# PSUM as one tile of eight banks and a new order of the same operations in a fused attention and MLP-mixer kernel

## The chip, the cores and the metric

One core of a Trainium2 chip runs the kernel. The metric is the device time of one execution in microseconds (us), the median over several runs. The engines are TensorE (PE, with its weight loads shown apart as PEld), VectorE (DVE), ScalarE (ACT), GpSimd (POOL) and SyncE (SP). Each works through its own list of instructions in order. DMA transfers are issued from POOL, SP and ACT.

## What is computed

Causal attention over blocks of 64 positions, then a mixer of tokens and channels, for 8 batches, 8 heads, 576 positions and 64 values per head (so a model width of 512):

```python
scores = scale * np.matmul(q, k.transpose(0, 1, 3, 2))     # block-causal mask: block_i >= block_j
attn = np.exp(scores - max); attn = attn / sum
x = np.matmul(attn, v)                                      # to (batch, 576, 512)
...
h = np.maximum(xt @ w_tok1, 0.0) @ w_tok2                   # over positions, 576 -> 256 -> 576
u = x + h.transpose(0, 2, 1)
h2 = np.maximum(u @ w_ch1, 0.0) @ w_ch2                     # over channels, 512 -> 1536 -> 512
return u + h2
```

Inputs and output are float32; the matmuls are in bfloat16.

## The kernel before

**The work.** For each batch the kernel makes `qT` and `kT` by 32x32 transposes on DVE, then for each half of the heads (`hg`, four heads) three score sets (`score_set`, L539, matmuls at L562), exponentials out of PSUM on ACT (L580 for two banks at once in the first batch, L736 and L777 for one bank), clears of masked parts (`clear`, L594, memset at L599) and a copy of the tail block (`tail`, L584), both on DVE or POOL. `head_out` (L605) multiplies by v for one head (L616) and divides on DVE (L636, L642); `ends_out` (L653) does the last 64 positions of two heads (L669, L691, L697). `token_up` (L805, L814 and L818) and `token_mix` (L888, L913 and L944), in the first batch `first_u` (L838), are the token mixer. The channel mixer's first product is plain for batch 0 (`channel_up`, L1041). For the other batches it saves one of eight block products (`channel_up_half` L1114, `channel_up_fast` L1238). There a first product goes to a bank, a copy on ACT or DVE (`seed`, through `cast` at L393 or L395) sets a second bank to the same values, and later products are added on in both. The second channel product is `first_down` (L1463) for batch 0 and `channel_down_fast` (L1372) for the rest; its results are added up by `fold` on DVE (L1396) and stored by SP or ACT (L1424 and L1438). The last 64 positions of all batches are gathered as one more batch, number 8, here called the mixed rows; its four stores are those of L1424.

**The order.** Nothing is scheduled at run time. `Plan.add` collects 1526 operations with their dependencies, and the table `ORDER` lists them as words: the operation's number, a letter for the engine (T, A, D, P, S), and, for a TensorE operation that opens banks, a letter for each place in PSUM. `Plan.placed` walks the table, and each operation issues its instructions on the engine named, so the table is the order on every engine. An operation that waits holds up all behind it on that engine.

**PSUM.** It has eight banks. Before, four are single tiles `mm` (letters a to d), and four are at first two pairs `sc` (s and t) that the first batch's score sets take whole. After the last exponential of the first batch the pairs are closed and reopened as four single tiles `late` (e to h). A bank's letter moves between named pools (`TURN`), which say whether the bank's last use wrote all of it (`covers`); a seeded bank that is not covered gets one more matmul (`cover`, L310).

**The start.** `raise_clock` (L358) runs 11 matmuls on zeros before anything has been loaded (L364), and then single filler matmuls, up to 37 of them, placed by the table where TensorE would wait (L372); 25 are in the table. POOL issues the loads of q, k and v of batch 0 (v in two halves, `load_v`, L456, one half for each four heads, in five pieces J of 128 positions, the last of 64), of batch 1's q and k (L417), of the token weights (`load_token_weights`, L477: `w1_sb` in two pieces, `w1o_sb`, `w2_sb`, issued at L480) and of the channel weights (L503, L512).

Of the kernel before, what the change touches and what calls it, by code (L numbers as in the profile page):

```python
# [9 lines left out]
FP32 = mybir.dt.float32  # L10
# [17 lines left out]
class Plan:  # L28


    TURN = {
        (pool, covers): to
        for pools in (("mm", "full"), ("late mm", "late"))
        for covers, to in zip((False, True), pools)
        for pool in pools
    }

    ENGINE = {"T": "PE", "A": "ACT", "D": "DVE", "P": "POOL", "S": "SP"}  # L40
    SLOTS = {
        **{letter: ("mm", n) for n, letter in enumerate("abcd")},
        **{letter: ("late", n) for n, letter in enumerate("efgh")},
        "s": ("sc01", 0), "t": ("sc23", 0),
    }

    def __init__(self):
        self.ops = []
        self.free = {}

    def pool(self, name, tiles):
        self.free[name] = list(range(len(tiles)))

    def add(
# [7 lines left out]
        o.emit, o.prio, o.take, o.give, o.xfer = emit, prio, take, give, xfer  # L62
# [6 lines left out]
    def bare(self, note):  # L69
        return note.get("seed", False) and note["pool"] in ("mm", "late mm")  # L70

    def placed(self):

        pool_of = {letter: pool for letter, (pool, _) in self.SLOTS.items()}
        held, done = set(), set()
        for word in ORDER.split():
            digits = word.rstrip("abcdefghstADPST")
# [4 lines left out]
            for letter, (pools, note) in zip(letters[1:], o.take):  # L82
                note["pool"], note["slot"], note["home"] = pool_of[letter], self.SLOTS[letter][1], letter
                assert letter not in held and note["pool"] in pools
                held.add(letter)
            yield o
            done.add(o.n)
            for note in o.give:
                if "home" not in note:
                    note["home"] = "efgh"[note["slot"]]  # L90
                else:
                    held.remove(note["home"])
                pool_of[note["home"]] = self.TURN.get((note["pool"], note.get("covers")), note["pool"])
# [4 lines left out]
    9D 8D 14S 7D 0A 15A 11S 41Ta 19P 69Tb 17P 1D 52Tb 21P 31P 25P 51Tb 65Tb 23P 29P 12A 27P 3D 2D 16D 20D 18D 22D  # L98
    13D 26D 24D 105Ts 106A 98Ttbc 61Td 57Td 49Td 99A 100D 30D 63Td 118A 122Ts 70Td 123A 78Td 62Td 54Td 102Tt 103A
# [79 lines left out]
def kernel(  # L179
# [82 lines left out]
    late = []  # L262

    P = Plan()
    SC = ("sc01", "sc23")
    for name in SC:
        P.pool(name, [0])
    P.pool("mm", mm)
# [1318 lines left out]
```

## Time and profile before

| | |
|---|---|
| timed runs | 283.83 us median of 3 (283.75 to 284.11) |
| span of the profiled execution, first to last instruction | 282.2 us |
| granted TensorE clock, mean | 1.000 |
| DVE idle | 282.2 - 238.8 = 43.4 us |
| DMA | 31.75 MB, mean 112 GB/s, of it 17.64 MB by POOL's queue |

The page gives the span of the profiled execution alone; its time with what lies around the span is not listed, and the timed runs are other executions. Matmul rows on the page overlap, because a matmul is pipelined and its end is modelled: a row of 0.38 us stands for a matmul that holds TensorE for less. In the chain of waits a row such as "53.72 0.97 PE mm L913 x4" gives the start, the time until the next piece, the engine, the tile, the line and the number of instructions. In the timeline a bracket gives the idle time ahead and what ended it.

### The profile page before, as it was taken

What the parts mean: (1) busy time and instruction counts of PE and PEld (TensorE: products, weight loads), DVE (VectorE), ACT (ScalarE), POOL (GpSimd) and SP (SyncE); (2) the same over time, 40 slices, a digit from 0 to 9 for tenths busy, and PEclk for the clock granted to TensorE, in tenths of its full rate; (3) what the DMA queues carried; (4) which work ended last, traced back from release to release, by engine and by line L of the source; (5) the groups of instructions that cost most, each with busy time, mean ns of one, the idle gap of its engine ahead of it and who ended that gap; (6) DMA issues with size and microseconds to landing.
All of it is one profiled execution on the core that took longest, in us unless ns stands there. A gap on an engine that the chain in (4) does not pass through costs nothing.

```text
span 282.2 us, 8544 instructions
## 1 busy us (share of the span) xinstructions
PE 275.3 (98%) x3580; PEld 193.2 (68%) x3580; DVE 238.8 (85%) x523; ACT 177.8 (63%) x326; POOL 78.8 (28%) x131
## 2 busy tenths in 40 slices
PE   7899999999999999999999999999999999999994
PEld 2457665475768877888776658744589664788884
DVE  4589598889889989999988879887797898898974
ACT  4788888775899774899997990326840858530000
POOL 8876726371613422092257210000000000000000
PEclk9999999999999999999999999999999999999999
DMA  8999999959958947699399465150127200020555
GB/s 160 167 153 194 191 200 203 162 63 170 95 88 229 150 67 56 151 104 127 46 118 161 31 141 120 42 114 19 37 49 210 80 0 0 3 75 14 212 126 174
DMA packets 64918, 31.75 MB, mean 112 GB/s; under 512 B 53104, under 2 KB 56176, under 8 KB 64880
## 3 DMA queue, kind: packets, MB, share of 16 engines
q0 software_dynamic: 45040, 17.64, 54.0%
q1 hardware_dynamic: 19408, 12.91, 16.7%
q10 hardware_dynamic: 432, 0.66, 0.7%
q8 instruction: 28, 0.46, 0.7%
q14 instruction: 10, 0.08, 0.1%
HBM read 35.85 MB, written 9.44 MB: 160 GB/s over the span
## 4 chain that ended last, share of the span: by engine, by line
PE 82%; DMA 10%; DVE 3%; ACT 2%; POOL 1%; issue 1%; DVEq 0%; POOLq 0%
PE mm L1372 13%; PE late L1372 11%; DMA qk_sb<-in_q_dram 7%; PE late L1114 7%; PE late L1238 6%; PE mm L1114 6%; PE mm L1238 6%; PE mm L562 4%; PE late L616 3%; DMA wc_sb<-in_moe_w_ch_dram 3%; PE late L562 3%; PE late L913 3%; PE mm L814 2%; PE mm L616 2%; PE late L814 2%; PE mm L913 2%
## 5 line engine op out<-in xcount | busy, mean ns | idle before, releaser
L777 ACT ACTIVATE e_sb<-mm 128x512 bf16<-128x512 f32 x94 | 53.5, 612 | 9.8 <-PE mm L562 4.2
L777 ACT ACTIVATE e_sb<-late 128x512 bf16<-128x512 f32 x74 | 43.0, 613 | 5.6 <-PE late L562 2.7
L440 DVE STREAM_TRANSPOSE qk_sb<-qk_sb 128x288 int32<-128x288 int32 (+2 forms) x57 | 38.3, 695 | 6.0 <-ACT qk_sb L393 1.9
L469 POOL DMA_DIRECT2D vals<-in_v_dram x45 | 37.1, 833 | 8.5 <-PE late L616 7.5
L1372 PEld LDWEIGHTS <-sums 128*128 128x128 bf16 x288 | 27.8, 98 | 4.2 <-issue 0.4
L1372 PEld LDWEIGHTS <-gT 128*128 128x128 bf16 x288 | 27.9, 98 | 3.7
L562 PEld LDWEIGHTS <-qk_sb 32*64 32x64 bf16 (+1 forms) x1024 | 16.9, 99 | 16.5 <-issue 9.6
L562 PE MATMUL mm<-qk_sb 32*64 32x320 bf16 (+6 forms) x534 | 27.7, 273 | 0.0
L616 PEld LDWEIGHTS <-e_sb 128*128 128x128 bf16 x640 | 23.9, 97 | 5.4 <-issue 0.9
L393 ACT COPY late<-mm 128x512 f32<-128x512 f32 (+1 forms) x14 | 8.0, 571 | 27.6 <-DVE o_sb L1396 14.5
L562 PE MATMUL late<-qk_sb 32*64 32x320 bf16 (+6 forms) x382 | 25.0, 277 | 0.3 <-DVE x_sb L642 0.3
L1114 PEld LDWEIGHTS <-ws_sb 128*128 128x128 bf16 x192 | 17.9, 98 | 4.2 <-issue 0.9
L599 POOL MEMSET e_sb<- 64x512 bf16 (+1 forms) x23 | 11.4, 511 | 31.7 <-ACT e_sb L777 28.4
L800 ACT ACTIVATE gT<-late 128x512 bf16<-128x512 f32 x20 | 12.2, 611 | 7.4 <-PE late L1114 4.9
L1114 PEld LDWEIGHTS <-wc_sb 128*128 128x128 bf16 x144 | 15.5, 113 | 1.8
L1238 PEld LDWEIGHTS <-ws_sb 128*128 128x128 bf16 x96 | 9.4, 98 | 9.8
L616 PE MATMUL late<-vals,e_sb 128*128 128x65 bf16 x360 | 15.8, 193 | 0.0
L642 DVE TENSOR_TENSOR x_sb<-late,rinv 128x256 bf16<-128x256 f32 x36 | 14.8, 418 | 0.7
L580 ACT ACTIVATE e_sb<-sc 128x1024 bf16<-128x1024 f32 x11 | 10.8, 1026 | 4.5 <-PE sc L562 4.5
L1372 PE MATMUL mm<-wd_sb,sums 128*128 128x256 bf16 x108 | 13.1, 273 | 0.0
L616 PE MATMUL mm<-vals,e_sb 128*128 128x65 bf16 x280 | 12.4, 193 | 0.0
L417 POOL DMA_DIRECT2D qk_sb<-in_k_dram x12 | 6.6, 551 | 20.7 <-ACT e_sb L777 7.1
(203 smaller groups left out, 649.4 us busy)
## 6 DMA issues: line engine op xcount, KB each, us to landing
out_dram<-o_sb SPq DMA_DIRECT2D x14, 512.0 KB, 3.0
vals<-in_v_dram POOLq DMA_DIRECT2D x28, 128.0 KB, 5.9
qk_sb<-in_k_dram POOLq DMA_DIRECT2D x12, 288.0 KB, 5.6
qk_sb<-in_q_dram POOLq DMA_DIRECT2D x12, 288.0 KB, 6.1
wc_sb<-in_moe_w_ch_dram POOLq DMA_DIRECT2D x8, 192.0 KB, 7.8
wc_sb<-in_moe_w_ch_dram POOLq DMA_DIRECT2D x3, 512.0 KB, 8.0
out_dram<-o_sb SPq DMA_DIRECT2D x4, 256.0 KB, 3.2
vals<-in_v_dram POOLq DMA_DIRECT2D x15, 64.0 KB, 5.4
```

Of the source, the lines that this page charges most:

```text
L440: nc.vector.transpose(dst[:, 0:S, :] .rearrange("p s e -> p (s e)") .bitcast(I32) .rearrange("p (a k) -> p k a", k=NB)[:, k0:k1], raw2.bit ...
L469: nc.gpsimd.dma_start(out=t[128 - p : 128, J, hs, 0:64], in_=src)
L562: nc.tensor.matmul(out=home(n)[rows, c : c + w], lhsT=kT[i][r, 64 * j : 64 * j + keys, par], rhs=qT[i][r, 64 * q : 64 * q + w, par], start ...
L599: (nc.vector if o.engine == "DVE" else nc.gpsimd).memset(late_keys, 0.0)
L616: nc.tensor.matmul(out=u[:, I, 0:65], lhsT=e[:, h, c : c + 128], rhs=vt[:, J, head, 0:65], start=(J == 0), stop=(J == I),)
L642: nc.vector.tensor_tensor(out=xt[:, 0:4, 64 * head : 64 * head + 64], in0=u[:, :, 0:64], in1=ri[:, 0:4].to_broadcast([128, 4, 64]), op=MULT,)
L777: nc.scalar.activation(dst, bank_of(x), EXP, scale=scale)
L800: nc.scalar.activation(dst, src, RELU)
L913: nc.tensor.matmul(out=bank_of(bank), lhsT=w2_sb[:, t, 128 * si : 128 * si + 128], rhs=at[:, t, :], start=(t == 0), stop=(t == NDT - 1),)
L1114: nc.tensor.matmul(out=bank_of(bank)[:, 256 * o_ : 256 * o_ + 256], lhsT=x(o_, m), rhs=y[:, :, m, :], start=opens, stop=m == 1, skip_group ...
L1238: nc.tensor.matmul(out=bank_of(bank), lhsT=x(m), rhs=y[:, :, m, :], start=first and m == 0, stop=m == 1, skip_group_check=not first,)
L1372: nc.tensor.matmul(out=bank_of(bank)[:, 256 * i : 256 * i + 256], lhsT=x[:, kk, 128 * i : 128 * i + 128], rhs=y[:, kk], start=first and i ...
```

## The change

The eight banks become one tile, `banks_sb`, 128 x 8 x 512. A place in PSUM is now a first bank (letters a to h) and a size, 1 or 2, so that the first batch's pairs can lie on any two neighbouring banks and are given back one use at a time; the pools, the closing of the pairs and its dependency on the last exponentials go. Whether a bank is covered is kept in one set.

```diff
     def bare(self, note):
-        return note.get("seed", False) and note["pool"] in ("mm", "late mm")
+        return note.get("seed", False) and not note["whole"]
...
-            for letter, (pools, note) in zip(letters[1:], o.take):
-                note["pool"], note["slot"], note["home"] = pool_of[letter], self.SLOTS[letter][1], letter
-                assert letter not in held and note["pool"] in pools
-                held.add(letter)
+            for letter, (size, note) in zip(letters[1:], o.take):
+                note["slot"] = "abcdefgh".index(letter)
+                banks = range(note["slot"], note["slot"] + size)
+                assert banks.stop <= 8 and not held.intersection(banks)
+                note["whole"] = self.covered.issuperset(banks)
+                held.update(banks)
             yield o
             done.add(o.n)
-            for note in o.give:
...
+            for note, lo, hi in o.give:
+                banks = range(note["slot"] + lo, note["slot"] + hi)
+                held.difference_update(banks)
+                (self.covered.update if note["covers"] else self.covered.difference_update)(banks)
...
-    13D 26D 24D 105Ts 106A 98Ttbc 61Td 57Td 49Td 99A 100D 30D 63Td 118A 122Ts 70Td 123A 78Td 62Td 54Td 102Tt 103A
+    22D 13D 26D 24D 105Te 106A 98Tgbc 82P 30D 99A 102Td 34P 125Tf 118A 32P 119A 28D 158Ta 103A 122Tc 126A 104D
...
-    mm = ring(4, [128, 512], FP32, "mm", psum)
-    held_banks = [tc.tile_pool(name="pairs", bufs=1, space=bass.MemoryType.PSUM)]
-    sc = ring(2, [128, 2, 512], FP32, "sc", held_banks[0].__enter__())
-    late = []
+    banks_sb = psum.tile([128, 8, 512], FP32, name="banks")
...
-    def bank_of(note):
-        if note["pool"] in EARLY:
-            return mm[note["slot"]]
...
+    def bank_of(note, i=0):
+        return banks_sb[:, note["slot"] + i]
...
-            nc.scalar.activation(dst, sc[SC.index(note["pool"])][:, :, 0:n], EXP, scale=scale)
+            nc.scalar.activation(dst, banks_sb[:, note["slot"] : note["slot"] + 2, 0:n], EXP, scale=scale)
```

The operations and their dependencies are the same 1526, but for the dependency on the closing of the pairs. The table is another one throughout: 21 of the 25 filler matmuls are no longer in it, 37 evacuations go from ACT to DVE and 31 from DVE to ACT, and 13 copies and clears go from DVE to POOL and 11 from POOL to DVE. All else keeps its engine. The counts of matmuls are the same apart from the fillers. Three places, on engines that wait or are waited for, are shown.

POOL at the start, from the second piece of batch 0's loads on. `vals` is v (`4x64` are four heads, 64 rows the last piece), `gT` holds batch 1's raw q and k, `w_sb` and `w1o_sb` are token weights. Before:

```order
L469 DMA vals<-in_v_dram 64x4x64
L469 DMA vals<-in_v_dram 128x4x64 x3
L417 DMA gT<-in_q_dram 128x1152
L417 DMA gT<-in_k_dram 128x1152 x2
L469 DMA vals<-in_v_dram 64x4x64
L469 DMA vals<-in_v_dram 128x4x64 x4
L480 DMA w_sb<-in_moe_w_tok_dram 128x4x256
L480 DMA w_sb<-in_moe_w_tok_dram 64x256
L480 DMA w1o_sb<-in_moe_w_tok_dram 64x256
L599 MEMSET e_sb 64x2x2x64
```

and now:

```order
L450 DMA w_sb<-in_moe_w_tok_dram 128x4x256
L387 DMA gT<-in_q_dram 128x1152
L439 DMA vals<-in_v_dram 64x4x64
L439 DMA vals<-in_v_dram 128x4x64
L563 MEMSET e_sb 64x2x2x64
L450 DMA w_sb<-in_moe_w_tok_dram 64x256
L563 MEMSET e_sb 64x2x2x64
L439 DMA vals<-in_v_dram 128x4x64 x2
L552 COPY vals<-e_sb 128x128
L439 DMA vals<-in_v_dram 128x4x64
L450 DMA w_sb<-in_moe_w_tok_dram 128x1152
```

The five pieces of the second half of v stood together ahead of the token weights; now they stand behind the large piece of them, apart from each other, with two clears and a copy between that wait for exponentials. Ahead of what is shown, `w1o_sb` now stands before the first half's later pieces, and the identity matrix (masks.py) before `w_sb`.

SP at the end, its stores to the output. `64x2x512` are stores of the mixed rows (256 KB each), `128x512` and `128x256` are stores of batch 7 (256 and 128 KB). Before:

```order
L1438 DMA out_dram<-o_sb 128x2x512 x7
L1424 DMA out_dram<-o_sb 64x2x512 x3
L1438 DMA out_dram<-o_sb 128x256
L1438 DMA out_dram<-o_sb 128x512
L1438 DMA out_dram<-o_sb 128x256 x2
```

and now:

```order
L1399 DMA out_dram<-o_sb 128x2x512 x6
L1385 DMA out_dram<-o_sb 64x2x512 x2
L1399 DMA out_dram<-o_sb 128x256
L1385 DMA out_dram<-o_sb 64x2x512
L1399 DMA out_dram<-o_sb 128x256 x2
L1399 DMA out_dram<-o_sb 128x512
```

The third store of the mixed rows moves behind the first store of batch 7, and the store of 128x512 from third last to last place.

ACT at the end, its three stores. Before:

```order
L393 COPY mm<-mm 128x512
L393 COPY late<-mm 128x256
L1424 DMA out_dram<-o_sb 64x2x512
L1438 DMA out_dram<-o_sb 128x512
L1438 DMA out_dram<-o_sb 128x256
```

and now:

```order
L1245 ACTIVATE vals<-vals 128x2x512
L363 COPY banks<-banks 128x256
L1385 DMA out_dram<-o_sb 64x2x512
L1399 DMA out_dram<-o_sb 128x256
L1399 DMA out_dram<-o_sb 128x512
```

The 256 KB store of batch 7 and the 128 KB store have changed places. In the table the last five words on TensorE are 1521, 1500, 1511, 1517 and 1496, six matmuls each (L1372). The last fold of the mixed rows stands just ahead of them, the fold of 1517 frees ACT's last store, and that of 1496 SP's last store.

224 lines of the change are left out of this document (94 added, 130 removed).

## The prediction

> **What bounds the kernel now.** I read the page's shares first, then the windows by stage, the chain of waits, and the timeline of the first 24 and the last 10 us.
>
> ```profile
> PE 275.3 (98%) x3580; PEld 193.2 (68%) x3580; DVE 238.8 (85%) x523; ACT 177.8 (63%) x326; POOL 78.8 (28%) x131
> 8.50:22.00 13.50, 13.38 (x251) 7.51 (x253) 9.86 (x33) 11.53 (x13) 10.53 (x19) 1.00 1.41 164
> 22.00:60.00 38.00, 37.59 (x650) 23.76 (x647) 31.99 (x83) 32.08 (x63) 19.59 (x34) 1.00 1.26 173
> 60.00:110.00 50.00, 50.00 (x768) 36.57 (x761) 46.44 (x107) 37.52 (x72) 18.67 (x28) 1.00 1.01 129
> 110.00:165.00 55.00, 54.69 (x984) 40.63 (x982) 50.29 (x122) 48.23 (x94) 21.62 (x35) 1.00 0.79 100
> 210.00:260.00 50.00, 50.00 (x379) 37.68 (x377) 43.61 (x70) 23.23 (x41) 0.00 (x0) 1.00 0.19 56
> ```
>
> The columns are PE, weight loads, DVE, ACT, POOL, then the granted clock, the DMA share and GB/s. TensorE is busy in every stretch, at clock 1.00. So four things make the time: when the first useful matmul starts, how much matmul work there is, what PE loses between, and what follows the last matmul. A busy PE hides its waits, so the losses are read from the chain, where one operation stands many times:
>
> ```profile
> 53.72 0.97 PE mm L913 x4
> 205.45 0.86 PE mm L913 x4
> 92.77 0.56 PE late L1114 x4
> 94.64 0.44 PE late L1114 x4
> 277.96 0.69 PE mm L1372 x6
> 278.67 0.42 DVE o_sb L1396
> ```
>
> A group that had to wait costs about 0.11 us more than the same group unblocked. Adding up, over the PE rows of the timeline, each operation's start-to-start time less that of the faster quarter of its kind, I estimate some 5 us of such losses from 22 to 165 us and 0.3 us from 165 us to the last matmul, which ends at 278.65. From there to the end are 282.2 - 278.65 = 3.55 us. In the first 22 us ACT sets the pace:
>
> ```profile
> 5.95 1.03 PE L372 MATMUL mm<-wd_sb 128*128 128x512 bf16 x4
> 7.86 0.88 PE L562 MATMUL sc<-qk_sb 32*128 32x512 bf16 x6 [0.89 <-DVE qk_sb L440]
> 8.53 1.94 ACT L580 ACTIVATE e_sb<-sc 128x1024 bf16<-128x1024 f32 x2 [3.67 <-PE sc L562]
> 10.47 0.49 ACT e_sb L736
> 17.77 0.56 PE sc L562 x4
> 19.91 1.02 ACT L580 ACTIVATE e_sb<-sc 128x1024 bf16<-128x1024 f32 x1 [0.52 <-PE sc L562]
> 20.24 0.77 PE L616 MATMUL mm<-vals,e_sb 128*128 128x65 bf16 x20
> 20.85 0.49 PE L372 MATMUL mm<-wd_sb 128*128 128x256 bf16 x2
> 22.53 0.38 PE L814 MATMUL mm<-x_sb,w_sb 128*128 128x128 bf16 x4 [0.19 <-DVE x_sb L642]
> 23.09 0.39 PE L814 MATMUL late<-x_sb,w_sb 128*128 128x128 bf16 x4
> L372 PE MATMUL mm<-wd_sb 128*128 128x512 bf16 (+1 forms) x25 | 6.3, 344 | 0.0
> L580 ACT ACTIVATE e_sb<-sc 128x1024 bf16<-128x1024 f32 x11 | 10.8, 1026 | 4.5 <-PE sc L562 4.5
> ```
>
> **The change part by part.** *One PSUM tile.* It adds and removes no instruction, and each operation still reads and writes its own bank: 0. *21 warming matmuls fewer.* Four stay ahead of 7.86; the other 21 of the 25 stood where PE had nothing ready. What covers them is that wait itself, so 0; at most the pair at 20.85 held up the next score set, so a gain up to 0.4. *VectorE.* 37 evacuations move from ACT to VectorE and 31 back, 13 tail operations go to POOL and 11 come back: four more on VectorE, at 238.8/523 = 0.46 us each about 2 us. Its 282.2 - 238.8 = 43 us of idle time hide them: 0, and 2 us where that cover is gone.
>
> *The first batch.* The score sets now stand close together and take any two free banks, so ACT need not starve. From 8.53, eleven wide exponentials at 1.94/2 = 0.97 and two small ones at 0.49 end at 20.2, where before the last ended at 20.93. The next batch's two score sets wait for banks freed by the last two exponentials and end at about 20.8 (0.56 for a set, as at 17.77); two token-up groups follow (23.09 - 22.53 = 0.56 each), and head 4, which needs the second half of v, is due at 22.0. With v at hand PE would be about 1 us ahead there: before reaches the end of its second token-up group at 23.09 + 0.56 = 23.65, having done two heads (0.77) and two end groups more and one score set (0.56) less. But v is late:
>
> ```profile
> 8.81 0.55 POOL L417 DMA_DIRECT2D gT<-in_q_dram  x1
> 10.11 0.54 POOL L417 DMA_DIRECT2D gT<-in_k_dram  x1 [0.75 <-DMA qk_sb<-in_k_dram]
> 11.51 3.60 POOL L469 DMA_DIRECT2D vals<-in_v_dram  x5 [0.17 <-issue]
> 15.06 0.79 POOL L480 DMA_DIRECT2D w_sb<-in_moe_w_tok_dram  x1
> 18.82 0.31 POOL L599 MEMSET e_sb<- 64x256 bf16 x1
> vals<-in_v_dram POOLq DMA_DIRECT2D x15, 64.0 KB, 5.4
> qk_sb<-in_q_dram POOLq DMA_DIRECT2D x1, 64.0 KB, 4.2
> ```
>
> Before, the five loads are issued from 11.51 to 15.11; 5.4 us after the last issue, at 14.4, is 19.8, and head 4 starts at 20.24. In the new order one more load stands ahead of the two 288 KB loads (8.81 and 10.11 become about 10.1 and 10.8), and then POOL issues the identity (0.5), the weights (0.79) and another q load (0.56) before v's first two pieces (1.4). Two clears follow that wait for the fifth wide and the second small exponential (8.53 + 5 x 0.97 + 2 x 0.49 = 14.4), with the small weight load between them (0.31, 0.54, 0.31 and gaps): about 16.2. Two pieces of v, a copy, and the last piece follow, which is issued near 18.2. It lands at 22.4 with the 4.2 us of the quickest such load, at 23.6 with the median. The heads behind it on PE wait 0.4 to 1.6 us, and so do the multiplications on VectorE, the token-up groups and the first channel groups that they feed. Against the lead of 1 us that is -0.6 to +0.6 at the head; but the lead itself is given up at the same chain (last head, multiply, token-up, add, transpose), which before also set the pace up to 30 us. I take +0.6, bounds -1.0 (the lead is kept) to +2.0 (nothing of the wait is hidden and the loads are slower).
>
> *The middle.* The work is the same and everything is in another place, so before's rows give bounds only. The nearest are the 5 us of losses: a better order gains 3 of them, a worse one loses 2 more. What tips it is the seeded products (L1114, L1238). A first product is copied to a second bank, and only then do its followers go on.
>
> ```profile
> L393 ACT COPY late<-mm 128x512 f32<-128x512 f32 x13 | 7.6, 588 | 13.1 <-PE mm L1238 12.8
> L1238 PE MATMUL mm<-e_sb,ws_sb 128*128 128x512 bf16 x38 | 10.8, 379 | 0.0
> ```
>
> The copy takes 0.59 us, and the first product's result stands 0.379 - 0.216 = 0.16 after its slot: 0.75 before any queue. Before, nearly all followers come three products later (3 x 0.43 = 1.29); now some ten come two later (0.86), which leaves 0.1 us for an engine that is 63 or 85% busy. At 0 to 0.2 each I take +0.3 for the middle, bounds -3 to +2.
>
> *The tail.* The last PE work is the same six matmuls and one fold. What goes out after it differs:
>
> ```profile
> 278.00:280.00 2.00, 0.63 (x6) 0.32 (x4) 0.84 (x2) 0.00 (x0) 0.00 (x0) 1.00 0.75 263
> 268.21 4.53 SPq L1424 DMA_DIRECT2D out_dram<-o_sb  x3
> 279.13 0.34 ACTq L1438 DMA_DIRECT2D out_dram<-o_sb  x1
> out_dram<-o_sb ACTq DMA_DIRECT2D x2, 256.0 KB, 4.3
> out_dram<-o_sb ACTq DMA_DIRECT2D x1, 128.0 KB, 1.7
> out_dram<-o_sb SPq DMA_DIRECT2D x4, 256.0 KB, 3.2
> ```
>
> Before, the mixed rows' four stores (L1424) have been issued by 272.9 and the last is a 128 KB store at 279.13 that lands in 1.7 us. Now two of those 256 KB stores follow a fold only four short products (0.66 each) before the end, and the last two stores are of 256 KB, one per queue, issued at the last matmul's end and 0.5 us after it. In the last 2.5 us of matmuls and behind them 1408 KB go out, before 640 KB. At 263 GB/s the 768 KB more take 2.9 us, the upper bound; a 256 KB store that lands in 2 us instead of 1.7 gives +0.3. By the median of 3.2 against 1.7 it is +1.5, less a little overlap: I take +1.2.
>
> Sum: 0.6 + 0.3 + 1.2 = +2.1 on the span of 282.2, 284.3. The runs' median, 283.83, is 1.63 above that span; kept, the forecast is 285.9.
>
> **The rivals.** *Faster, a smoother middle:* ACT is nearly 2 us ahead after the first batch, and 3 of the 5 us from 22 to 165 go; with +0.2 from the start and +0.8 from the tail the span is 280.2, the time 281.8. For it: the losses come in quanta of 0.11 at hundreds of places. Against it: the followers that come closer. It decides if v's last piece lands before 22.4. *No change:* v is in time, the middle gains 1, the tail costs 1.2: about 284. *VectorE or the copies become the bound:* VectorE is 46.44 of 50 us busy from 60 to 110; if its 2 us more and the close followers show in full, the middle costs +2.3 instead of +0.3: 287.9. *The clock drops:* the 21 matmuls kept PE busy between 9 and 21 us.
>
> ```profile
> 1.66 4.45 PE L364 MATMUL mm<-wd_sb 128*128 128x512 bf16 x11 [1.66 <-DVE wd_sb L339]
> ```
>
> These eleven first matmuls took 4.45 us, 0.40 each against 0.86/4 = 0.216 later: a start at reduced rate costs 4.45 - 2.4 = 2.1 us. If the new gaps bring that back once, the time is 288.0. I see gaps of up to 1.8 us (score sets issued by 10.2, the next transposes done at 12.0), with work between them. The Trainium skill, page "TensorE: Matmul & The Clock Gate", section "Why this matters for your kernels", warns of PE gaps over some 3 us between bursts. By that rule gaps of this length keep the clock; no row of before shows a gap that long.
>
> **How the numbers follow.** A measurement of this kernel can tell 0.2%, 0.57 us, from no change. Forecast 0.48, with its own range 284.4 to 287.4; VectorE or the copies 0.14; the clock 0.06; no change 0.14; faster 0.18. Slower is 0.48 + 0.14 + 0.06 = 0.68. The faster case reaches below 282.6 and the two dear ones beyond 288.3 in about 1 in 10 each, so the range is 282.6 to 288.3.
>
> **What would show it.** Start: head 4's second half begins near 23.6 with PE idle ahead of it, and POOL issues the last piece of v near 18.2. Middle: the L913 and L1114 groups of 0.97 and 0.56 as often as before or more. Tail: the span ends about 4.7 us after the last matmul, and the last 256 KB store lands 3 us or more after its issue. Clock: any stretch after 8.5 below 1.00. The forecast is wrong if v's last piece has landed by 22.4, if the tail stays at 3.6 us, or if the losses from 22 to 165 fall below 3 us.

## The result and the profile after

The changed kernel takes 303.41 us (302.72 to 305.33, 4 runs) against 283.97 before (283.75 to 284.26, 4 runs): ratio 1.0694, 95% interval 1.0656 to 1.0733. It is 19.4 us slower. The forecast was 285.9 in a range of 282.6 to 288.3: right in sign, far off in size. One execution each of e2 (303.28 us) and e13 (309.35 us) ran more than 1.5% slower than the fastest of its kernel and is left out of the table below.

The page of the changed kernel: the span, the engines' busy time, PE's busy tenths and granted clock in 40 slices, the chain by engine.

```profile
span 300.8 us, 8507 instructions
PE 279.8 (93%) x3559; PEld 195.6 (65%) x3559; DVE 243.6 (81%) x527; ACT 175.6 (58%) x320; POOL 78.9 (26%) x133
PE   7899999999986499979999999999999999999991
PEclk9959999999999699999999999999999999999997
PE 78%; DVE 10%; DMA 6%; issue 2%; ACT 2%; DVEq 0%
```

Before, PE was 98% busy; now there is a hole in the 13th and 14th slice and a smaller one in the 18th, with a drop of the clock behind the first hole and another in the third slice. A transfer stands in the chain of waits with 6%. The windows around the holes (PE, weight loads, DVE, ACT, POOL, then clock, DMA share, GB/s), PE's waits (us in total, times, longest), and the pieces of the chain there:

```profile
80.00:90.00 10.00, 8.94 (x139) 6.37 (x137) 9.42 (x24) 8.30 (x18) 6.17 (x9) 1.00 0.65 79
90.00:100.00 10.00, 5.17 (x96) 4.03 (x94) 5.65 (x16) 5.63 (x11) 0.89 (x1) 0.98 2.16 120
100.00:110.00 10.00, 7.79 (x84) 5.62 (x85) 6.03 (x10) 3.94 (x8) 1.50 (x3) 0.68 0.97 41
130.00:140.00 10.00, 8.01 (x106) 6.86 (x104) 6.81 (x19) 7.24 (x15) 4.01 (x7) 1.00 1.27 135
```

```profile
PE banks L1075 <- DMA uT<-u_sb: 8.8, 2, 7.0
```

```profile
89.95 12.21 DMA uT<-u_sb
102.21 1.04 PE banks L1075 x4
...
128.01 6.64 DMA uT<-u_sb
```

From 96 us on all engines are idle together until 102 us, waiting for one transfer. It is a transpose through DMA. `token_mix` leaves u, the result of the token mixer, in `u_sb`; two transposing DMAs on SP's queue (L980 before, L941 now), one for each half, turn it into `uT`, the operand of the channel products (L1114 before, L1075 now). The first of batch 2 was issued at 85.42 and took 9.1 us; the second was issued at 89.95 and was 12.2 us on its way; that of batch 3 took 6.6. The landing times of all the transposes, before and then after:

```profile
DMA to landing us min/median/max: 3.0/3.2/4.6
```

```profile
DMA to landing us min/median/max: 3.2/5.6/12.2
```

What went on meanwhile is in the timeline of SP and of POOL, first after:

```profile
85.42 6.81 SPq L941 DMA_TRANSPOSE uT<-u_sb  x2
```

```profile
84.02 1.10 POOL L387 DMA_DIRECT2D qk_sb<-in_q_dram  x2 [0.83 <-DVE rinv L600]
85.10 0.55 POOL L563 MEMSET e_sb<- 64x512 bf16 x1
85.57 3.54 POOL L439 DMA_DIRECT2D vals<-in_v_dram  x4
89.06 0.61 POOL L387 DMA_DIRECT2D qk_sb<-in_k_dram  x1
94.70 0.89 POOL L439 DMA_DIRECT2D vals<-in_v_dram  x1 [5.03 <-PE banks L580]
```

and the same places before:

```profile
84.19 3.00 SPq L980 DMA_TRANSPOSE uT<-u_sb  x2
```

```profile
79.83 0.52 POOL L599 MEMSET e_sb<- 64x512 bf16 x1 [1.53 <-DVE vals L588]
89.33 0.52 POOL L599 MEMSET e_sb<- 64x512 bf16 x1 [8.97 <-ACT e_sb L777]
89.84 0.53 POOL L417 DMA_DIRECT2D qk_sb<-in_k_dram  x1
```

Before, POOL sat 9 us in front of a clear that waited for ACT, and the queue behind it was still; in that quiet the two transposes went through in 3.2 us. Now POOL issues four 128 KB pieces of v and a 288 KB piece of k from 85.6 to 89.7, and the second transpose comes right behind them. What the DMA engines moved from 93 to 95 us, packets and MB by queue (q0 is POOL's, q1 SP's), and what SP's queue moved from 84 to 103 us:

```profile
DMA packets 2342, 0.29 MB, mean 147 GB/s; under 512 B 2342, under 2 KB 2342, under 8 KB 2342
q0 software_dynamic: 2336, 0.29, 298.6%
q1 hardware_dynamic: 6, 0.00, 1.1%
```

```profile
q1 hardware_dynamic: 2112, 0.52, 36.4%
```

From 93 to 95 us the pieces of v move, in packets that are all under 512 B, and six packets of SP's queue. The 2112 packets are those of the two transposes, 1056 each. Of them 1056 moved before 95 us and 1056 after, so the six are the end of the first transpose (landed at 94.5), and the second, issued five us earlier, had not moved a packet by 95.

**The end** is longer too. The chain's last piece shows the last matmul at 267.09 + 27.52 = 294.6, so 6.2 us to the end of the span, against 3.55 before:

```profile
267.09 27.52 PE banks L1333 x252
```

**Two numbers for each run.** The time from the program's start to the first channel product of batch 0 (below: start) varies between executions of one and the same kernel, so the runs are compared by what lies behind it as well (below: rest, span less start). The start is read from the line of the tile `uT`, here for two executions of the changed kernel, 29.8 and 31.3 us:

```profile
L1002 PE MATMUL banks<-uT,wc_sb x48: 376/379/407, 29.8 to 46.3; 128*128 128x512 bf16 x48
```

```profile
L1002 PE MATMUL banks<-uT,wc_sb x48: 376/379/407, 31.3 to 47.8; 128*128 128x512 bf16 x48
```

| kernel | median us (lowest to highest, runs) | start | rest |
|---|---|---|---|
| before | 283.97 (283.75 to 284.26, 4) | 29.9 | 252.3 |
| changed | 303.41 (302.72 to 305.33, 4) | 29.8 | 271.0 |
| changed, again (e17) | 303.90 (302.95 to 305.95, 4) | 31.3 | 271.5 |
| e1 one tile, old order | 285.09 (284.13 to 285.84, 10) | 30.1 | 253.3 |
| e2 five loads behind | 299.05 (296.79 to 300.72, 3) | 30.1 | 267.1 |
| e4 before, loads early | 285.02 (1) | 29.9 | 253.3 |
| e5 u early | 298.33 (1) | 31.3 | 265.1 |
| e6 four pieces of v behind | 295.65 (294.47 to 296.25, 4) | 31.8 | 260.9 |
| e7 fillers back | 302.91 (301.37 to 304.50, 4) | 32.0 | 267.5 |
| e8 end | 307.81 (1) | 34.9 | 271.0 |
| e9 batch 3 | 301.84 (1) | 32.1 | 267.9 |
| e10 four edits | 294.79 (294.36 to 295.04, 4) | 32.0 | 260.3 |
| e11 e10, old first part | 296.80 (295.83 to 298.06, 4) | 29.9 | 265.0 |
| e12 before, new first part | 290.67 (289.65 to 291.65, 4) | 32.3 | 256.1 |
| e13 changed, old first part | 304.27 (303.89 to 306.03, 3) | 30.8 | 273.4 |
| e14 middle mended, old end | 290.88 (290.01 to 293.24, 4) | 32.4 | 257.3 |
| e15 before, new end | 288.18 (287.96 to 289.54, 4) | 30.2 | 256.0 |
| e16 e14, token weights back | 292.02 (291.26 to 292.67, 4) | 33.5 | 257.2 |
| e18 clear back on POOL | 297.65 (297.20 to 298.07, 4) | 32.4 | 263.1 |
| e19 before, clear on DVE | 284.49 (284.15 to 285.31, 9) | 30.1 | 252.5 |

The changed kernel's rest is 18.7 us longer than before's.

### The profile page after: what moved, and what is told of

Read it like the earlier page. It is cut to its first block, busy times and chain, and to the rows that moved or that the text cites. A ratio compares the mean times of both kernels' runs of the same rounds, so it can differ in the third digit from the quotient of the medians.

```text
span 300.8 us, 8507 instructions
## 1 busy us (share of the span) xinstructions
PE 279.8 (93%) x3559; PEld 195.6 (65%) x3559; DVE 243.6 (81%) x527; ACT 175.6 (58%) x320; POOL 78.9 (26%) x133
## 4 chain that ended last, share of the span: by engine, by line
PE 78%; DVE 10%; DMA 6%; issue 2%; ACT 2%; DVEq 0%
PE banks L1333 23%; PE banks L1199 12%; PE banks L1075 10%; PE banks L526 8%; DMA uT<-u_sb 6%; PE banks L775 5%; PE banks L1424 4%; PE banks L580 4%; PE banks L1002 3%; PE banks L874 3%; DVE qk_sb L410 3%; DVE x_sb L606 2%; PE banks L334 2%; ACT e_sb L544 2%; DVE u_sb L889 1%
## 5 line engine op out<-in xcount | busy, mean ns | idle before, releaser
L738 ACT ACTIVATE e_sb<-banks 128x512 bf16<-128x512 f32 x168 | 87.4, 613 | 33.1 <-PE banks L526 31.9
L363 ACT COPY banks<-banks 128x512 f32<-128x512 f32 (+1 forms) x44 | 25.0, 574 | 37.0 <-PE banks L1333 15.3
L526 PE MATMUL banks<-qk_sb 32*64 32x320 bf16 (+6 forms) x1024 | 36.8, 286 | 3.5 <-DVE u_sb L889 1.0
L606 DVE TENSOR_TENSOR x_sb<-banks,rinv 128x256 bf16<-128x256 f32 x64 | 26.8, 421 | 1.7
L761 ACT ACTIVATE gT<-banks 128x512 bf16<-128x512 f32 x38 | 22.6, 610 | 8.8 <-PE banks L1199 3.5
L580 PE MATMUL banks<-vals,e_sb 128*128 128x65 bf16 x640 | 25.5, 195 | 0.1
L1333 PE MATMUL banks<-wd_sb,sums 128*128 128x256 bf16 x192 | 23.1, 273 | 0.0
L1075 PEld LDWEIGHTS <-wc_sb 128*128 128x128 bf16 x144 | 15.4, 114 | 11.7 <-DMA uT<-u_sb 9.4
L1075 PEld LDWEIGHTS <-ws_sb 128*128 128x128 bf16 x192 | 18.0, 98 | 4.3 <-issue 0.9
L1199 PE MATMUL banks<-e_sb,ws_sb 128*128 128x512 bf16 x72 | 20.2, 379 | 0.0
L1114 DVE TENSOR_TENSOR gT<-banks,half 128x512 bf16<-128x512 f32 x24 | 15.9, 685 | 5.0 <-PE banks L1075 3.5
L1075 PE MATMUL banks<-uT,wc_sb 128*128 128x256 bf16 x72 | 11.0, 281 | 8.8 <-DMA uT<-u_sb 8.8
L1333 PE MATMUL banks<-wc_sb,gT 128*128 128x256 bf16 x144 | 18.8, 283 | 0.0
L1333 PE MATMUL banks<-wd_sb,gT 128*128 128x256 bf16 x144 | 17.7, 273 | 0.0
## 6 DMA issues: line engine op xcount, KB each, us to landing
qk_sb<-in_k_dram POOLq DMA_DIRECT2D x12, 288.0 KB, 5.9
qk_sb<-in_q_dram POOLq DMA_DIRECT2D x12, 288.0 KB, 5.6
out_dram<-o_sb SPq DMA_DIRECT2D x4, 256.0 KB, 3.3
```

The lines of the kernel that those rows point to most:

```text
L363: nc.scalar.copy(dst, src)
L526: nc.tensor.matmul(out=bank_of(*homes[n])[rows, c : c + w], lhsT=kT[i][r, 64 * j : 64 * j + keys, par], rhs=qT[i][r, 64 * q : 64 * q + w, ...
L580: nc.tensor.matmul(out=u[:, I, 0:65], lhsT=e[:, h, c : c + 128], rhs=vt[:, J, head, 0:65], start=(J == 0), stop=(J == I),)
L606: nc.vector.tensor_tensor(out=xt[:, 0:4, 64 * head : 64 * head + 64], in0=u[:, :, 0:64], in1=ri[:, 0:4].to_broadcast([128, 4, 64]), op=MULT,)
L738: nc.scalar.activation(dst, bank_of(x), EXP, scale=scale)
L761: nc.scalar.activation(dst, src, RELU)
```

## The experiments

All edits but the first are moves of words in `ORDER`: a number is an operation, T, A, D, P, S its engine. In the diffs "..." stands for words left out.

### The tile alone (e1)

Before's order with all fillers in the changed code; the pairs s and t become banks e, f and g, h.

```diff
-    13D 26D 24D 105Ts 106A 98Ttbc 61Td 57Td 49Td ...
+    13D 26D 24D 105Te 106A 98Tgbc 61Td 57Td 49Td ...
```

> The order of before, operation for operation and with all fillers, in the code with one PSUM tile of eight banks (the old double-bank slots become banks e,f and g,h). Theory 1 (the loss sits in the new order, in the transposes of u that land late behind GpSimd's loads): the tile itself costs nothing, 284.0 us, between 283.5 and 284.6, and the wait of TensorE for uT stays as before, under 0.5 us. Rival (one tile ties reads and writes of different banks together and makes engines wait): a good part of the 19.4 us shows here, 288 us or more.

Measured: 285.09 us, ratio 1.0026 (1.0005 to 1.0048), 0.1 to 1.4 us. The tile is not quite free, but not 19 us: the loss sits in the order.

### The loads of v behind the transposes (e2, e6)

In e2 four pieces of v of batch 4 (698, 700, 699, 697) and a piece of k of batch 5 (854) go behind the next load on POOL's queue, 867, which waits for TensorE. In e6 only the pieces of v do.

```diff
-    ... 484Tfe 485Th 698P 693D ... 497T 700P 588D ... 503Ted 699P 717A ... 704A 697P 635Tch ... 867P 627A
+    ... 484Tfe 485Th 693D ... 497T 588D ... 503Ted 717A ... 704A 635Tch ... 867P 698P 700P 699P 697P 627A
```

> The changed kernel with five of GpSimd's loads (four 128 KB pieces of v of batch 4, one 288 KB piece of k of batch 5) moved behind the next load on the same queue, which waits for TensorE until about 94 us; nothing else moved. Theory 1 (these loads fill the DMA engines while the two transposes of u of batch 2 are under way): the second transpose lands within 5 us of its issue instead of 12.2, TensorE's wait for uT in the products of batch 2 falls from 7.2 us to under 1, and of the 8.9 us that 90 to 110 us lost against before nearly all comes back: 294.5 us, between 293 and 296. Rival 2 (VectorE makes u too late, the loads don't matter): time above 301 us, the landing still at 10 us or more. Rival 3 (the moved loads come too late for batch 4 and become the next wait): uT on time, but a new wait in the attention products of batch 4, 297 to 301 us.

> The changed kernel with only the four 128 KB pieces of v of batch 4 moved behind the next load on GpSimd's queue (issued near 95 us instead of 85.6 to 88.2); the piece of k of batch 5 stays ahead of the transposes, because with it moved too VectorE waited for it and TensorE lost 3.1 us at 107 us. Theory 1 (the pieces of v ahead of the second transpose hold it up): the first product of batch 2 starts without a wait for uT (7.2 us before), no stall over 1 us at 107 us, span 291.5 to 293.5 and time 293 to 295.5 us where the clock is as in the changed kernel. Rival (VectorE's late u decides): the wait at the first product of batch 2 stays above 3 us, time 298 us or more.

Measured in e2: no stall at the first product of batch 2, but one of 3.0 us at 107 us:

```profile
PE banks L524 <- DVE gT L761: 3.0, 1, 3.0
```

In VectorE's list two transposes of the moved piece of k stand ahead of the operation that PE waited for. So a part of the gain was lost again to the moved load's own lateness, as rival 3 had it: 299.05 us, the rest 4 us shorter instead of 9. In e6, with k in its place:

```profile
86.72 0.55 POOL L385 DMA_DIRECT2D qk_sb<-in_k_dram  x1
95.44 4.41 POOL L437 DMA_DIRECT2D vals<-in_v_dram  x5 [8.17 <-PE banks L578]
```

```profile
90.00:100.00 10.00, 9.87 (x190) 8.15 (x188) 9.56 (x25) 8.36 (x17) 4.41 (x5) 1.00 1.00 117
100.00:110.00 10.00, 9.95 (x124) 7.85 (x124) 8.65 (x15) 5.45 (x11) 1.55 (x3) 1.00 1.09 149
```

From 90 to 110 us PE is busy 19.8 of 20 us against 13.0, and the clock stays up. The second transpose lands in 3.7 us; the first, with the pieces of q and k still around it, takes 7.6 but is not waited for. The rest falls from 271 to 260.9: four moved loads are worth 10 us. The median shows 7.8 of them, as the start came 2 us later in e6 than in the first profile of the changed kernel.

### u earlier instead (e5)

```diff
-    606Ta 692D ... 484Tfe 485Th 698P ... 563Td 607D 561D ... 490T 608Ta 486D ... 709Tdfhg 609D
+    606Ta 607D 692D ... 484Tfe 485Th 608Ta 609D 698P ... 563Td 561D ... 490T 486D ... 709Tdfhg
```

> The changed kernel with the second pair of token-mixing products and VectorE's scaling of them (the last two quarters of u of batch 2) moved forward by 1 to 3 us; the loads stay where they are. Theory 1 (loads and transposes share the DMA engines): the second transpose is issued near 88.2 us instead of 89.95 but still lands near 100 us, 10 us or more after its issue; 301 to 303.5 us. Rival 2 (VectorE's lateness is the cause): the wait for uT falls by 5 us or more, 293 to 298 us.

Measured: 298.33 us in one run. Theory 1's numbers were wrong, and the rival's wait came true, its time nearly. The transpose was issued at 89.28, 0.7 us sooner, or 1.8 us against the loads, which stand 1.1 us later in this execution; so it went ahead of the 288 KB piece of k instead of behind it:

```profile
89.28 8.62 DMA uT<-u_sb
```

It took 8.6 us instead of 12.2, and the first product of batch 2 waited 0.4 us instead of 7.0. That fits a transpose that waits for the loads issued ahead of it. It shows as well that the lateness of u matters: with the loads where they were, u made earlier brings 6 us of the rest (271.0 to 265.1), of the 10 that e6 brings with u as late as ever. Either edit alone takes most of the collision away. In the changed kernel the last quarters of u were scaled at 86.8 and 89.26, before at 84.56 and 85.25.

```profile
86.80 0.68 DVE L889 TENSOR_TENSOR u_sb<-banks,x_sb 128x512 bf16<-128x512 f32 x1
89.26 0.66 DVE L889 TENSOR_TENSOR u_sb<-banks,x_sb 128x512 bf16<-128x512 f32 x1
```

```profile
84.56 0.68 DVE L928 TENSOR_TENSOR u_sb<-late,x_sb 128x512 bf16<-128x512 f32 x1
85.25 0.66 DVE L928 TENSOR_TENSOR u_sb<-mm,x_sb 128x512 bf16<-128x512 f32 x1
```

### The fault put into the kernel before (e4)

```diff
-    ... 691P ... 694P 567D ... 857P 586A ... 575P 593Te ... 713A 712A 714P ... 854P ... 697P 699P ... 698P
+    ... 691P ... 567D ... 586A ... 575P 694P 857P 593Te ... 713A 712A 854P 697P 699P 698P 714P ...
```

> The kernel before with six of GpSimd's loads (three of 288 KB, three of 128 KB) moved so that they are issued between 80 and 86 us, around the two transposes of u of batch 2 at 84 to 86 us. Theory 1: these transposes now take 6 us or more from issue to landing instead of 3.2, and as the products need them 6.8 us after the second issue, TensorE waits 0 to 4 us: 284 to 288 us. Rival 2 (loads don't slow transposes): landing stays at 3.2 to 4 us and the time at 284.

Measured: 285.02 us in one run, and the second transpose slowed as theory 1 said, from 3.2 to 7.8 us:

```profile
86.37 7.81 DMA uT<-u_sb
```

```profile
PE late L1115 <- DMA uT<-u_sb: 1.2, 1, 1.2
```

Similar traffic costs 1.2 us there and 7 in the changed kernel: there the transfer takes 7.8 us and the product follows 6.8 us behind its issue; in the changed kernel it takes 12.2, and the product is due 5.2 us behind.

### Why the loads ran into the transposes (e18, e19)

In the table of the changed kernel most of these loads stand behind the transposes; POOL still issued them first, because nothing in its list waited. Before, a clear (714) of a probability tile stood ahead of them on POOL; it waits for four exponentials and held POOL until 89.33. In the changed order it is one of the clears that went to VectorE. e18 puts it back; e19 takes it from POOL in the kernel before.

```diff
-    ... 485Th 698P 693D ... 711A 593Tb ... 745A 746A 714D 744A
+    ... 485Th 693D ... 711A 714P 698P 593Tb ... 745A 746A 744A
```

> The changed kernel with one clear of a probability tile (batch 4) done on GpSimd again instead of VectorE, ahead of the loads of v of batch 4, and one of these loads moved behind it so that all stand behind it as before; all else as changed. If the clear was the gate that held the loads back: GpSimd waits in it until about 92 us for ACT, the loads start behind it, the first product of batch 2 has no wait over 1 us (7.2 in the changed kernel), and from the start of the channel products to the end it takes 260 to 262 us instead of 271; time 294 to 297 us. Rival (the loads reach the transposes anyhow): the wait stays above 4 us, 300 us or more.

> The kernel before with the same clear on VectorE instead of GpSimd, all words in their places. If it is the gate: GpSimd issues the piece of k and the pieces of v from 80.4 us on instead of 89.8, the transposes of batch 2 (84.2 and 85.9) take over 4 us to land instead of 3.2, up to 8, and as they have 6.8 us of slack the time rises by 0 to 1.5 us, 284 to 285.5. Rival: the loads stay where they were, landing 3.2 us, 284.0.

Measured in e18: 297.65 us, the rest 263.1, and no wait at the first product of batch 2. POOL stands in the clear until 94.3, and the loads follow:

```profile
94.32 0.59 POOL L561 MEMSET e_sb<- 64x512 bf16 x1 [6.48 <-PE banks L1073]
94.86 3.52 POOL L437 DMA_DIRECT2D vals<-in_v_dram  x4
```

The one clear is worth 8 us of the rest (two us less than e6; 1.1 of these are a longer wait at batch 3, 2.3 us against 1.2). In e19 the loads did go ahead, at 81.6, but three of them only. The first transpose, of 84.85 us, landed in 4.3 us and the second in 3.4, instead of 3.2 each, and PE did not wait for uT: 284.49 us, 0.4 to 1.1 us more than before. The expected slowing, over 4 us, thus showed in one of the two and barely; the time is as expected. Losing the gate is not enough; the loads must also be under way when the transposes are issued.

### Batch 3 (e9)

The transpose of the row means (784), which now stood between the two of u, goes back to a later place, and two loads (951, 868) go behind the second transpose.

```diff
-    ... 951P 517S ... 868P ... 877P 657A 784S ... 866P 765Ta ... 1050S
+    ... 517S ... 877P 657A ... 866P 951P 868P 765Ta ... 784S 1050S
```

> The changed kernel with the transpose of the row means of batch 3 moved 55 us later on SyncE's queue, and two loads (288 KB of k, 128 KB of v) moved behind the second transpose of u of batch 3. Theory 1: that transpose lands within 4.5 us of its issue instead of 6.6, TensorE's second wait for uT (2.0 us at 134.7) falls below 0.5, span 1.5 to 2 us shorter. Rival (u of batch 3 is late on VectorE, the traffic doesn't matter): the wait stays at 1.5 us or more.

Measured: PE's second wait for uT is gone (before the edit 8.01 of 10 us busy from 130 to 140):

```profile
130.00:140.00 10.00, 9.80 (x131) 8.77 (x130) 8.59 (x24) 8.87 (x17) 7.38 (x12) 1.00 1.29 162
```

The rest is 3.1 to 3.6 us shorter, about 2 of it by this wait; the start was 2.3 us later in this execution, so the span fell by 0.8 only.

### The end (e8, e14, e15)

e8 moves the two products that end in 256 KB stores ahead of the last three. e14 takes the last 16 us of all engines from before, over a middle mended as in e6 and e9. e15 puts the new order of the last 15 us into the kernel before.

```diff
-    1478T 1479D 1483S 1521T 1522D 1525S 1482A 1500T 1501D 1511T 1512D 1517T 1491D 1503S 1504A 1496T 1518D 1523A 1497D 1502S
+    1511T 1512D 1491D 1517T 1518D 1523A 1496T 1497D 1502S 1478T 1479D 1483S 1521T 1522D 1525S 1482A 1500T 1501D 1503S 1504A
```

> The changed kernel with the last products in another order: the two that end in 256 KB stores ahead of the three that end in 128 KB stores. Theory: the last store sets the tail, so the time from the last matmul to the end falls from 6.2 us to 3.5 to 4.3 us; span about 2.3 us shorter. Rival (the tail is the mass of stores in the last 8 us, whatever comes last): 5.5 us or more remain.

> The changed kernel with the four pieces of v behind the transposes, the transpose of the row means and two loads behind the second transpose of batch 3, and the last 16 us of all engines in the order of before. If the order of the stores at the end costs 2.6 us: the last matmul to the end takes 3.4 to 4.2 us instead of 6.2, and the time is 2 to 4 us under the 295.65 with v alone: 291.5 to 293.5 us. Rival (the end is long because the middle is late or because the stores pile up from further back): 5 us or more remain, 294.5 us or more.

> The kernel before with the last 15 us of all engines in the new order. If the order of the stores at the end costs 2.6 us: the last matmul to the end takes 5.8 to 6.6 us instead of 3.6 and the time is 286 to 287.2 us. As predicted (1.2 us): 284.9 to 285.5 us. Rival (the end follows from what comes ahead of it): 284 us.

e8 missed its expectation: 7.2 us from the last matmul to the end instead of 3.5 to 4.3. By moving the last store's product forward it pushed another with 512 KB of stores (1478) to the end. In e14 and e15 the last matmuls and the stores' issues are:

```profile
258.56 27.57 PE banks L1331 x252
```

```profile
275.69 4.53 SPq L1383 DMA_DIRECT2D out_dram<-o_sb  x3
281.32 5.02 SPq L1397 DMA_DIRECT2D out_dram<-o_sb  x4
```

```profile
270.46 9.35 PE banks L1332 x84
```

```profile
277.28 0.60 SPq L1384 DMA_DIRECT2D out_dram<-o_sb  x1
277.97 3.44 SPq L1398 DMA_DIRECT2D out_dram<-o_sb  x3
```

e14: 289.7 - 286.1 = 3.6 us, as before. e15: 286.2 - 279.8 = 6.4, as in the changed kernel; its rest is 256.0 against 253.3 for the tile alone. So the order of the last 15 us is worth 2.7 us by itself, more than the 1.2 forecast; e15's time, 288.2, lies above what was expected of it, as the tile comes on top. Which store comes last does not set it (e8). Six profiles fit the mass of stores that go out with the last matmuls: the two 256 KB stores of 1478 are issued 6.4 us or more ahead of the last matmul's end before and in e14 (3.6 us to the end of the span), 3.2 ahead in e10 (5.4), 2.5 in the changed kernel (6.2) and in e15 (6.4), and 0.6 in e8 (7.2). No run varies the mass alone.

### The first part (e7, e11, e12, e13, e16, e17)

e7 puts the 21 fillers back. e11 and e13 take the first 46 us from before, e12 puts the new first 47 us into the kernel before (without fillers), e16 puts the token weights behind v again in e14, e17 is the changed kernel once more.

```diff
-    ... 98Tgbc 82P 30D 99A 102Td 34P 125Tf 118A ... 158Ta 103A 122Tc ...
+    ... 98Tgbc 82P 30D 99A 102Td 61Ta 57Ta 49Ta 34P 125Tf 63Ta 70Ta 118A ... 158Ta 78Tc 62Tc 103A 122Tc 54Te 45Te 50Te ...
```

> The changed kernel with the 21 warming matmuls back, between its first products of 9 to 20 us. If the missing fillers let the clock drop to 0.5 at 14 to 21 us: the granted clock is 1.0 from 8 us on, and the spread over runs (302.7 to 305.3) shrinks to about 1 us. For the time: fillers cost 21 x 0.22 = 4.7 us of TensorE and the half clock cost 3.7 us, so nothing is won if TensorE sets the first batch (303 to 305 us); if the fillers fit into its idle time at 9 to 15 us, 300 to 302.5 us. Rival (the drop comes from elsewhere, the fillers don't matter): clock still 0.5 at 14 to 21 us.

> The same four edits, and the first 46 us (all engines, with the 21 fillers) in the order of before. The first part of the new order started the channel products at 29.8 to 34.9 us in the profiles so far, before at 29.9. If that is a cost of the new first part: 1 to 3 us under the run with the four edits alone, 287 to 290 us, all runs within 1 us, granted clock 1.0 up to 46 us. Rival (the first part costs nothing): the same time as with the four edits, within 0.5 us.

> The kernel before from 47 us on, with the first 47 us (all engines, 21 fillers fewer, token weights ahead of the second half of v) in the new order. If the new first part costs: clock 0.5 between 14 and 22 us, 285 to 288 us, runs spread over 1.5 us or more. If the missing fillers are free, as predicted: 283.5 to 284.5 us. If they are won: under 283.3 us.

> The changed kernel with its first 46 us in the order of before, nothing else changed. If the new first part costs 1 to 3 us: 300.5 to 302.5 us, with less spread than the 302.7 to 305.3 of the changed kernel; the wait for uT of batch 2 stays at about 7 us. Rival (it costs nothing): 303 to 304 us.

> The kernel with the mended middle and the old end (290.9 us), with the three loads of token weights moved back behind the second half of v on GpSimd's queue. If the place of the weights delays the first part: the channel products start near 30 us instead of 32.4 and the time falls by 1.5 to 2.5 us, to 288.4 to 289.4. If the weights are needed where they now stand: TensorE waits for them at the first token products near 22 us, start at 32.5 us or later, 291 us or more. Rival (the start varies for another reason): start between 30 and 34 and time between 290 and 293 us.

> The changed kernel once more. If the start of the channel products varies from run to run in one kernel: it is not at 29.8 us again but between 30 and 35, with runs from 302 to 306 us and the longer the later it starts. Rival (the start belongs to the kernel): 29.8 us and 302.5 to 303.5.

The windows from 14 to 22 us, of the changed kernel and of e7:

```profile
14.00:22.00 8.00, 7.78 (x111) 4.80 (x107) 6.32 (x21) 6.84 (x10) 5.81 (x13) 0.57 1.40 163
```

```profile
14.00:22.00 8.00, 6.63 (x106) 3.73 (x107) 4.54 (x14) 6.59 (x7) 6.54 (x14) 1.00 1.44 167
```

The fillers do hold the clock, 1.00 against 0.57, but the times cannot be told apart: 302.91 us against 303.41, intervals that overlap, and as wide a spread. The start came no earlier with the clock held, 32.0 us against 29.8 and 31.3. (The rest in e7's profile is 3.5 us shorter, about 3 of it because the first product of batch 2 waited 3.9 us instead of 7.0: the size of that collision moves with what comes ahead of it.) e16 answers for the token weights: behind v again they are waited for (1.1 us by the waits of PE), the start is 33.5 and the time 292.0 against 290.9. So nothing shows that their new place costs. e11, e12 and e13 all came out slower than expected (296.8, 290.7 and 304.3 us against 287 to 290, 285 to 288 and 300.5 to 302.5) and don't settle more: where two orders are joined, PE waits 2 to 4 us behind 47 us for VectorE and ACT, more than the first part's own effect. What all profiles together show is the start: 29.8 to 34.9 us with the new first part (eleven profiles with neither fillers nor weights moved, median 32.0), 29.9 to 30.8 with the old one (seven). So the new first part costs about 2 us at the median, and up to 5. In the late ones PE stands still in the middle of one group, here in e10:

```profile
28.07 0.28 PE L631 MATMUL banks<-vals,e_sb 128*64 128x65 bf16 x6 [1.48 <-issue]
```

It waits for nothing that the profile shows. The instruction queue (q8) gives a hint: in every profile of the new first part without fillers it moves one packet of 0.02 MB shortly before. Where that packet moves before 25 us, the stop in this group is 0.8 us at most (the changed kernel, e17, e2, e5); where it moves later, 1.2 to 1.9 us. Late instructions would look like this, but no run tests it, and it accounts for less than 2 of the up to 5 us. The rest stayed open.

### Four edits together (e10)

e6, e5 and e9 and the product of the 512 KB of stores (1478) ahead of the last eight.

> The changed kernel with four edits together: the four pieces of v behind the transposes (alone 7.8 us), the last two quarters of u of batch 2 scaled earlier, the transpose of the row means and two loads behind the second transpose of batch 3, and the product that releases 512 KB of stores moved ahead of the last eight products. If the loss of the middle and the end is what these waits show, their prices add: 303.4 less 7.8, less 0.5 to 1 for u, less 1.9 for batch 3, less about 1.5 for the end: 290 to 292.5 us. The last matmul to the end takes 4 to 5 us instead of 6.2. Rival (the waits reappear elsewhere): 294 us or more.

Measured: 294.79 us, only 0.9 under e6. The waits for uT are gone, but e5's edit brings two new stalls of 0.4 and 0.7 us at 91 and 92 us, and the end still takes 5.4 us. The prices did not add. The best of all mended versions is e14 at 290.9; none beats the kernel before.

## Why the prediction was wrong, point by point

**The step that failed** is the middle: "+0.3 for the middle, bounds -3 to +2". The bounds came from the 5 us of losses that before's rows show, and the terms from how close the followers of seeded products come. Where the forecast adds 0.3 us, the rest less the end grew by some 16 us (18.7 - 2.65), and the runs show 12 of them: 10 for the transposes of batch 2 (e6), about 2 for those of batch 3 (e9). "The work is the same and everything is in another place" was true and the wrong thing to bound: before's small losses say what its order costs, not what another order can cost. No term of the prediction stands for the queues of SP and POOL in the middle. The quiet in which before's transposes went through could have been read in before's timeline (POOL idle 8.97 us, SP's transposes inside it, 3.2 us to landing against 4.9 to 6.1 for loads of 128 and 288 KB when others are under way), and the clear that made it is one of those that the change moves.

**VectorE, 0 "where its idle time hides them".** The count was right, four more instructions, but they and the rest came to 4.8 us more of busy time (243.6) instead of 2; 57 us stayed idle, and it did not become the bound. But idle time in the sum hides nothing at one place: u of batch 2 was ready 4 us later than before, and without that the collision loses most of its price (e5).

**One tile, 0:** 0.7 us, 0.1 to 1.4 (e1); a small term, slightly mis-sized.

**21 fillers, 0, "a gain up to 0.4":** no run contradicts it (e7). The clock did fall, which the rival put at 288.0 us; that price does not show in e7 against the changed kernel, and the first part seems not to follow TensorE's speed there. The rival's 2.1 us were read from the eleven first matmuls as a start at reduced rate, though before's granted clock is 1.00 from 0 to 8.5 us.

**The first batch, +0.6 (-1.0 to +2.0).** The argument fell: POOL issued v's last piece at 16.7 instead of 18.2, it landed 5.3 us later, and head 4 at 22.8 did not wait. The cost, +2 at the median and 0 in the profiled execution, falls within the bounds by luck: its reason stayed open.

**The end, +1.2 (+0.3 to +2.9):** +2.65 in the profile, 2.7 in e15. The direction was right, and the size came near its upper bound, which was reckoned by bytes and bandwidth; the medians of before were the wrong guide for seven stores at once: SP's stores of 128 KB now land in 4.5 us at the median, before in 1.8.

**The rivals.** Of the clock the rival had the place right, the price wrong, and gaps of up to 1.8 us that are not there (0.3 at most ahead of the drop); the drop behind the 7 us hole, 0.68 from 100 to 110 us, is a consequence of the hole. That a transfer might come late in the middle was not among them.

**What stays open:** some 5 us of e14's rest against before (257.3 to 252.3, at most 1.4 of it the tile), which no run divides further, and the start.

## What to carry to other kernels

When an order changes, follow every DMA that the critical engine waits for through three questions: what is issued ahead of it on all queues, what held that back until now, and how much slack the consumer leaves. An instruction that waits on a queue can be the gate that keeps bulk loads away from a short urgent transfer; moving it to another engine opens the gate, though the instruction itself takes 0.5 us. An engine's idle time in the sum covers nothing; slack is read at the place.

## What the runs showed of the hardware that was not expected

**A transfer that takes 3.2 us alone took 12.2 among others' loads.** What kept the second transpose of batch 2 from moving a packet before 95 us can be the pieces of v or the first transpose ahead of it on SP's own queue, which ended at 94.5; the packets do not separate the two. Without the pieces of v it landed in 3.7 us (e6). The Trainium skill, page "DMA: Bandwidth & Descriptors", section "Queues, rings and completion order", says that each DMA engine takes turns between queues packet by packet. This trace does not decide on that rule: from 89 to 93 us both queues move (1024 packets of SP's, 737 of POOL's), and from then on only six packets of SP's are known to have been ready; when the second transpose's descriptors were is not visible.

**The clock falls without a long gap.** In the changed kernel PE is busy 5.14 of 6 us between 8 and 14 us, no idle stretch in it is longer than 0.3 us, and the clock then is at half for 7 us. With the fillers (e7) it stays at 1.00, though PE is hardly busier, 5.27 us; here the longest gap after, then both windows:

```profile
10.52 0.61 PE L526 MATMUL banks<-qk_sb 32*128 32x512 bf16 x3 [0.30 <-ACT e_sb L544]
8.00:14.00 6.00, 5.14 (x114) 2.89 (x111) 4.00 (x10) 5.47 (x7) 5.64 (x11) 1.00 1.42 173
8.00:14.00 6.00, 5.27 (x92) 2.47 (x94) 3.79 (x9) 4.80 (x7) 5.82 (x11) 1.00 1.40 161
```

The prediction leaned on the rule in the Trainium skill, page "TensorE: Matmul & The Clock Gate", section "Why this matters for your kernels", that gaps over some 3 us bring the lower clock. Here the clock fell without such a gap, and the busy time of the window does not tell the two kernels apart either. What differs in the rows is the fillers themselves, matmuls of the form 128x128 (`128*128`) among others that are mostly `32*128` or `32*64`. That their form is the reason is not shown.

**The pieces of v move slowly.** All in packets under 512 B, they moved at 147 GB/s from 93 to 95 us with the DMA engines busy throughout; by an estimate from that rate 128 KB take about 0.9 us. Before's stores, in packets over 2 KB, moved at 341 to 423 GB/s between 88.4 and 90 us. The former are loads and the latter stores, so the size of the packets is not shown to be the cause.
